# Gated linear attention and a hard-swish MLP in float32: signs of the second weight's slices taken by ScalarE, and a new order of all instructions

## The chip, the cores and the metric

The kernel runs on one core of a Trainium2 chip. The core has TensorE (PE in the profile) for matrix products, VectorE (DVE), ScalarE (ACT), GpSimd (POOL), and SyncE (SP), whose queue issues the transfers here. The metric is the device time of one execution in microseconds. The median of three runs of the kernel before is 535.52 us (535.26 to 536.10).

## What is computed

For every batch and head a 48 by 48 state decays row by row with alpha, takes in the outer product of k and v, and is read by q. The result, 3072 tokens of 384 numbers, goes through two weights with a hard-swish between them.

```python
batch, n_heads, seq, head_dim = (4, 8, 768, 48)
n_tokens, d_model, d_ff = (3072, 384, 2048)
...
for t in range(S):
    state = alpha[:, :, t, :, None] * state + np.einsum('bhd,bhe->bhde', k[:, :, t], v[:, :, t])
    y[:, :, t] = np.einsum('bhd,bhde->bhe', q[:, :, t], state)
...
x = np.ascontiguousarray(attn_out.transpose(0, 2, 1, 3)).reshape(B * S, H * D)
h = x @ w_in
relu6 = np.clip(h + 3.0, 0.0, 6.0)
g = h * relu6 / 6.0
return (g @ w_out).astype(np.float32)
```

The weights arrive as float64, that is as pairs of 32-bit words, and are made float32 on the chip.

## The kernel before

**Attention.** The sequence is cut into 24 chunks of 128 tokens (six for each batch). Chunk j has its loads `la`, `lk`, `lq`, `lv`; transposes `ta`, `tk`, `tq` (by TensorE for j below 6, by VectorE from then on); `ca` puts alpha in place; `r` and `p` are VectorE's scans that make the decay factors; `k` and `q` multiply by them. `kb` and `ck` turn k to token order (from chunk 8 on `kt`, `kw`, `kr` do it through memory), `sc` are the scores, `m` masks them, `qa` and `sv` place q and the state as extra rows, `u` is TensorE's update of the state, `sm` and `st` add it and decay it, `ya` and `yb` are the two halves of the output, `cy` copies it out as input for the MLP.

**The MLP.** Two chunks make a group of 256 tokens, twelve groups in all. Groups 0 and 1 use the weights as they are: `f`, or `fa` and `fb` for one chunk, is the first product, `fr` the clip on ScalarE, `fg` the multiplication on VectorE, `b` the second product in four parts (for group 0), `bo` and `so` its way out. From group 2 on the first product is formed from sums (`xc` of inputs, `y` of the first weight) in 20 products `M`, with `n`, `o`, `e`, `h` behind them; the second product is from group 1 on made of 7 products `P`, from sums `s` of its input and `x` of the second weight, with `K`, `G` and the store `O` behind them. `x.0` to `x.3` need all eight slices of the second weight; `P.1.3` reads what `x.1` writes, `P.1.2` what `x.2` writes. `z` are idle products of the identity matrix with itself.

**The weights.** Both come in 16 slices of 768 numbers for each of 128 partitions (768 KB each): 0 to 7 are the first weight, 8 to 15 the second. `w` loads a slice into one of five buffers of word pairs; three of these hold slices 8 to 15 in turn, so a later load waits until an earlier slice's `d4` has run. Then there are two ways (lines 173 to 217):

- Slices in `BY_HALVES` (0, 1, 2 and 4 before): ScalarE's `d1` rounds the low word, `dx` writes a float16 zero with the number's sign into the upper half of the low word, `d2` takes the magnitude times 2^16; VectorE's `d3` clamps it and shifts it left by 3; GpSimd's `d4` adds the low word.
- The other twelve: `d1` and `d2` without the factor, no `dx`; `d3` has a third step on VectorE (line 210) that combines sign and top bits of the high word with the shifted bits; `d4` adds the low word to that.

**The order.** Nothing orders the work but one string of some 1790 words, each a step, worked off by `run` (line 748 and on). Every engine, and SP's queue of transfers, takes its own instructions in the order of these words, and waits for what other engines must have finished.

Of the kernel before, what the change touches and what calls it, by code (L numbers as in the profile page):

```python
# [17 lines left out]
def kernel(  # L18
# [42 lines left out]
    G = 2  # L61
# [114 lines left out]
    BY_HALVES = {0, 1, 2, 4}  # L176
# [395 lines left out]
    for i in range(8):  # L572
        r, o = divmod(i, 3)
# [176 lines left out]
    with tc.manual_schedule():  # L750
        run("""z.0.5 z.0.3 z.0.1 z.0.8 qa.0.0 w.0 d2.0 d3.0 la.0 ta.0.0 ca.0 r.0 lk.0 tk.0.1 k.0
               z.0.2 p.0 la.1 ta.1.2 lq.0 tq.0.3 ca.1 r.1 lk.1 lv.0.0 sv.0.0 d1.0 kb.0.0 ck.0 z.0.2
               u.0.2.1 sm.0.0 sv.0.1 q.0 qa.0.1 tk.1.0 k.1 p.1 z.0.2 sc.0.2.3 m.0 la.2 ta.2.0 ca.2
               dx.0 w.2 d2.2 kb.1.0 ck.1 lq.1 r.2 sm.0.1 st.1 tq.1.2 q.1 d3.2 z.0.3 d1.2 dx.2 lv.1.1
               u.1.3.1 sv.1.0 sm.1.0 p.2 sm.1.1 sc.1.0.2 m.1 ya.0.3 yb.0 cy.0 lq.2 w.1 d1.1 tq.2.1
               q.2 d4.2 lk.2 tk.2.3 k.2 fa.2.0 d4.0 st.2 sc.2.0.2 d2.1 d3.1 m.2 dx.1 d4.1 qa.1.1
               lk.3 la.3 ta.3.1 ca.3 la.4 fa.0.1 sv.1.1 w.3 r.3 ta.4.3 ca.4 r.4 tk.3.1 k.3 kb.2.0
               qa.1.0 d2.3 ya.1.2 yb.1 cy.1 fa.1.2 lq.3 ck.2 d1.3 p.3 d3.3 lv.2.2 u.2.3.2 sm.2.0
               d4.3 fb.2 tq.3.1 q.3 fb.1 qa.2.0 sm.2.1 sv.2.0 st.3 fr.0.2.0 fg.0.2 lk.4 tk.4.0
               sv.2.1 w.5 d2.5 k.4 d3.5 d1.5 qa.3.0 d4.5 qa.2.1 sc.3.1.3 m.3 w.6 d2.6 d1.6 d3.6 d4.6  # L760
               lv.3.0 lq.4 w.7 kb.3.2 fb.0 f.0.3.3 kb.4.0 ya.2.1 ck.3 u.3.3.2 sm.3.0 fr.0.3.1 fg.0.3
               fr.0.1.0 fg.0.1 qa.3.1 sv.3.0 sm.3.1 p.4 d2.7 sv.3.1 d1.7 d3.7 d4.7 f.0.5.0 fr.0.5.1
               fr.0.0.0 fg.0.5 fg.0.0 tq.4.3 ck.4 la.5 ta.5.2 f.0.6.3 ca.5 w.4 d2.4 ya.3.0 yb.3 cy.3
               fr.0.6.1 yb.2 cy.2 w.9 d2.9 q.4 qa.4.1 d1.4 d1.9 dx.4 la.6 w.8 d3.4 r.5 lk.5 w.10
               d3.9 p.5 ca.6 fg.0.6 d4.9 w.12 lq.5 lv.4.1 d2.8 d3.8 f.0.7.2 d1.8 st.4 d4.8 d4.4 w.11
               fr.0.7.0 fg.0.7 f.1.7.0 fr.1.7.1 fg.1.7 sc.4.0.2 m.4 f.1.1.1 fr.1.1.0 fg.1.1 f.1.3.3
               fr.1.3.1 d2.10 d1.10 tk.5.3 f.1.0.2 d2.12 d3.10 d4.10 w.13 fg.1.3 fr.1.0.0 fg.1.0 k.5
               d3.12 lq.6 f.1.6.0 f.1.2.1 u.4.1.0 sm.4.0 d1.12 d4.12 sv.4.0 qa.4.0 ya.4.2 fr.1.6.1
               fg.1.6 w.15 tq.5.3 fa.4.3 sv.4.1 d2.11 kb.5.1 d2.13 fr.1.2.0 f.1.4.2 fr.1.4.1 d1.11
               sm.4.1 q.5 r.6 d3.11 d3.13 fg.1.4 d4.11 lv.5.0 lk.6 tq.6 p.6 d2.15 d3.15 fg.1.2 d1.13  # L770
               d4.13 sc.5.0.3 yb.4 f.1.5.0 fr.1.5.1 fg.1.5 tk.6 m.5 b.1.0.2 fb.4 b.1.1 d1.15 d4.15
               st.5 y.5 w.14 la.7 lk.7 cy.4 d2.14 qa.5.1 ck.5 b.0.0.1 fr.0.4.0 d3.14 k.6 q.6 ca.7
               fg.0.4 d1.14 d4.14 x.0 y.1 y.10 b.0.1 y.0 y.2 u.5.2 P.1.0.0 K.1.0 qa.5.0 sv.5.0
               qa.6.1 P.1.1.3 b.0.2 b.1.2 kb.6.0 ya.5.3 y.6 s.1.0.0 sm.5.0 sv.5.1 G.1.0.0 tk.7
               s.1.1.1 s.1.2.3 x.1 yb.5 cy.5 b.1.3 sc.6.1.2 lv.6.2 ck.6 u.6.3.0 s.1.3.2 x.2 P.1.2
               b.0.3 K.1.1 y.7 s.1.4 s.1.5 y.11 y.3 r.7 xc.2.1 x.3 y.4 y.8 xc.2.3 k.7 xc.2.0 xc.2.4
               y.9 y.12 y.16 y.13 y.15 P.1.3.3 K.1.2 P.1.4 bo.1 P.1.5 xc.2.5 G.1.1.1 P.1.6 y.14 y.17
               y.19 xc.2.6 sm.6.0 G.1.2.2 y.20 M.2.0.2 lv.12.1 la.8 O.1.1 O.1.0 ca.8 y.18 y.21 y.23
               so.1 G.1.3.3 n.2.0.8 bo.0 lq.7 lv.7.0 O.1.2 m.6 xc.2.2 xc.2.10 xc.2.7 tq.7 r.8 p.7
               xc.2.8 sv.6.1 M.2.15.3 M.2.1 kb.7.3 n.2.1.9 M.2.16 M.2.2 n.2.2.10 M.2.7.0 n.2.7.11  # L780
               sm.6.1 xc.2.9 q.7 p.8 M.2.3 M.2.4 n.2.4.12 M.2.8 o.2.0.0 M.2.5 n.2.5.13 qa.7.0 sv.6.0
               st.7 lk.8 O.1.3 lq.8 lk.9 la.9 la.10 tk.8 tq.8 lq.10 lq.9 ya.6.1 yb.6 M.2.9 z.1.3
               M.2.18.1 o.2.1.0 e.2.1.1 M.2.10 cy.6 ck.7 sc.7.0.2 u.7.1.3 n.2.10.14 M.2.11 qa.7.1
               ca.9 la.11 y.22 M.2.6.2 h.2.1 q.8 m.7 e.2.0.0 h.2.0 n.2.11.15 qa.6.0 n.2.18.10 qa.8.1
               M.2.12 M.2.19 n.2.12.12 M.2.13 sm.7.0 sv.7.1 r.9 k.8 o.2.3.0 sv.7.0 ya.7.0 y.24
               o.2.5.0 n.2.13.12 o.2.2.0 yb.7 cy.7 sc.8.1.2 xc.3.1 o.2.2.1 e.2.2.1 xc.3.3 o.2.3.1
               M.2.14 xc.3.4 xc.3.0 xc.3.5 o.2.4.0 xc.3.7 xc.3.6 o.2.6.0 P.2.0.1 M.3.0.2 M.2.17
               h.2.2 o.2.6.1 e.2.3.0 h.2.3 o.2.7.0 K.2.0 n.3.0.12 M.3.1 n.3.1.9 e.2.5.1 M.3.7.0
               n.3.7.13 xc.3.8 o.2.7.1 xc.3.2 kt.8 e.2.6.0 h.2.6 tk.9 M.3.2 n.3.2.10 e.2.4.0 P.2.1.3
               h.2.4 h.2.5 s.2.0.14 e.2.7.0 G.2.0.1 h.2.7 M.3.3 M.3.4 n.3.4.8 k.9 s.2.1.11 M.3.8  # L790
               o.3.0.0 ca.10 kt.9 P.2.3.3 s.2.2.15 s.2.3.14 lv.8.2 kw.8 kr.8 lk.10 sm.7.1 xc.3.9
               M.3.5 n.3.5.11 K.2.2 e.3.0.1 xc.3.10 M.3.9 o.3.1.0 P.2.2 K.2.1 u.8.0.3 M.3.18.2 s.2.5
               M.3.10 n.3.10.14 n.3.18.15 e.3.1.0 s.2.4 P.2.4 tq.9 h.3.0 st.8 sv.8.0 M.3.11 n.3.11.8
               tk.10 p.9 sm.8.0 q.9 r.10 k.10 qa.9.0 qa.9.1 m.8 sm.8.1 h.3.1 M.3.19 o.3.5.0 kt.10
               P.2.5 G.2.2.0 st.9 M.3.12 sc.9.0.1 qa.8.0 n.3.12.10 o.3.3.0 kw.9 lv.9.0 kr.9 sv.8.1
               u.9.2.3 sm.9.0 sv.9.1 sv.9.0 G.2.1.2 sm.9.1 st.10 M.3.15.2 M.3.16 M.3.6.3 M.3.13 m.9
               o.3.4.0 o.3.6.0 tq.10 n.3.13.10 o.3.2.0 e.3.4.1 ya.8.2 yb.8 ya.9.3 yb.9 cy.9 M.3.14
# [135 lines left out]
```

## Time and profile before

| what | value |
|---|---|
| median of three runs | 535.52 us |
| the profiled execution | 535.44 us |
| its span in the trace | 533.7 us |
| granted TensorE clock over the span | 1.0 |
| transfers | 54.40 MB, mean 102 GB/s |
| VectorE's clamps and shifts of the full path, lines 207 and 208 | 12 and 12, mean 703 and 605 ns |
| clamps and shifts of the path by halves, lines 203 and 205 | 4 and 4, mean 860 and 696 ns |
| ScalarE's rounding and magnitude, lines 186 and 196 | 935 and 929 ns |
| idle products, line 532 | 58 instructions for 29 pairs |

Times are counted from the start of the span. A float32 product of TensorE is two instructions, so 29 idle pairs are 58. Busy time of TensorE contains overlapped and modelled ends, so work is better counted from start to start. TensorE's first 34 instructions, idle products, begin at 1.46 and take 6.75 us; later ones follow each other at about 0.11.

### The profile page before, as it was taken

What the parts mean: (1) busy time and instruction counts of PE and PEld (TensorE: products, weight loads), DVE (VectorE), ACT (ScalarE), POOL (GpSimd) and SP (SyncE); (2) the same over time, 40 slices, a digit from 0 to 9 for tenths busy, and PEclk for the clock granted to TensorE, in tenths of its full rate; (3) what the DMA queues carried; (4) which work ended last, traced back from release to release, by engine and by line L of the source; (5) the groups of instructions that cost most, each with busy time, mean ns of one, the idle gap of its engine ahead of it and who ended that gap; (6) DMA issues with size and microseconds to landing.
All of it is one profiled execution on the core that took longest, in us unless ns stands there. A gap on an engine that the chain in (4) does not pass through costs nothing.

```text
span 533.7 us, 15143 instructions
## 1 busy us (share of the span) xinstructions
PE 524.6 (98%) x6306; PEld 499.4 (94%) x6306; DVE 477.2 (89%) x849; ACT 257.2 (48%) x503; POOL 50.4 (9%) x71
## 2 busy tenths in 40 slices
PE   8799999999999999999999999999999999999997
PEld 7698886789999999999999999999999999999997
DVE  6999989999999999998999999999999899496382
ACT  3889865212653553553544444642634544553340
POOL 5333425100000000000000000000000000000000
DMA  9998876005615155254344355044454042100001
GB/s 174 217 252 256 215 216 152 21 2 154 152 30 116 32 121 135 57 140 95 87 110 113 91 124 140 19 120 102 115 136 104 11 110 43 44 2 2 15 16 37
DMA packets 124100, 54.40 MB, mean 102 GB/s; under 512 B 83328, under 2 KB 116864, under 8 KB 124032
## 3 DMA queue, kind: packets, MB, share of 16 engines
q1 hardware_dynamic: 124032, 53.44, 42.5%
q8 instruction: 49, 0.80, 0.6%
q14 instruction: 19, 0.16, 0.1%
HBM read 44.50 MB, written 8.91 MB: 100 GB/s over the span
## 4 chain that ended last, share of the span: by engine, by line
PE 85%; DVE 8%; POOL 2%; DMA 2%; ACT 1%; issue 1%; SPq 1%; DVEq 0%; POOLq 0%
PE m_ps L703 34%; PE m_ps L600 34%; PE m_ps L478 5%; PE t_ps L455 4%; PE t_ps L346 2%; PE t_ps L429 2%; PE m_ps L489 2%; PE t_ps L282 1%; DVE rings L647 1%; DMA v<-in_v_dram 1%; DVE raw L537 1%; ACT raw L191 1%; DMA kq<-in_k_dram 1%; DVE g_sb L647 1%; DVE w L537 1%
## 5 line engine op out<-in xcount | busy, mean ns | idle before, releaser
L606 ACT COPY g_sb<-m_ps 128x512 f32<-128x512 f32 x110 | 63.6, 584 | 124.9 <-PE m_ps L600 104.1
L703 PE MATMUL m_ps<-w,g_sb 128*128 128x192 f32 x704 | 121.7, 327 | 0.0
L703 PEld LDWEIGHTS m_ps<-w,g_sb 128*128 128x128 f32 x704 | 113.7, 190 | 0.4
L703 PE MATMUL m_ps<-rings,g_sb 128*128 128x192 f32 x528 | 91.5, 326 | 0.0
L703 PEld LDWEIGHTS m_ps<-rings,g_sb 128*128 128x128 f32 x528 | 85.4, 190 | 0.1
L600 PE MATMUL m_ps<-xc,w 128*128 128x128 f32 x640 | 82.7, 277 | 0.3 <-DVE w L541 0.3
L600 PEld LDWEIGHTS m_ps<-xc,w 128*128 128x128 f32 x640 | 77.5, 192 | 1.5 <-issue 0.5
L494 ACT ACTIVATE r<-g_sb,half 128x512 f32<-128x512 f32 x80 | 56.8, 722 | 32.9 <-DVE g_sb L541 12.1
L498 DVE SCALAR_TENSOR_TENSOR g_sb<-r,g_sb 128x512 f32<-128x512 f32 x80 | 53.6, 682 | 4.6 <-ACT r L494 4.2
L600 PE MATMUL m_ps<-xT,raw 128*128 128x128 f32 x400 | 52.5, 277 | 0.0
L600 PEld LDWEIGHTS m_ps<-xT,raw 128*128 128x128 f32 x400 | 48.6, 192 | 0.6
L409 POOL TENSOR_TENSOR st<-sm,R 128x192 f32<-128x192 f32 x20 | 12.9, 643 | 353.8 <-DVE sm L439 306.7
L647 DVE TENSOR_TENSOR g_sb<-g_sb 128x512 f32<-128x512 f32 (+1 forms) x55 | 42.0, 795 | 0.2
L600 PE MATMUL m_ps<-xT,w 128*128 128x128 f32 x320 | 42.0, 276 | 0.0
L600 PEld LDWEIGHTS m_ps<-xT,w 128*128 128x128 f32 x320 | 39.3, 192 | 0.1
L366 ACT COPY A<-q 48x256 f32<-48x256 f32 x88 | 35.5, 404 | 5.0 <-DVE q L332 3.7
L356 DVE TENSOR_TENSOR A<-t_ps,mask 64x256 f32<-64x256 f32 x96 | 36.0, 414 | 0.4
L478 PE MATMUL m_ps<-xT,w 128*128 128x256 f32 x144 | 32.8, 382 | 0.0
L600 PE MATMUL m_ps<-xc,raw 128*128 128x128 f32 x240 | 31.8, 276 | 0.0
L309 DVE TENSOR_TENSOR_SCAN R<-t,ones 128x516 f32<-128x516 f32 x24 | 29.7, 1236 | 1.1 <-ACT t L300 1.0
L478 PEld LDWEIGHTS m_ps<-xT,w 128*128 128x128 f32 x144 | 26.7, 190 | 3.6
L600 PEld LDWEIGHTS m_ps<-xc,raw 128*128 128x128 f32 x240 | 29.6, 192 | 0.1
(104 smaller groups left out, 731.0 us busy)
## 6 DMA issues: line engine op xcount, KB each, us to landing
raw<-in_moe_w_out_dram SPq DMA_DIRECT2D x8, 768.0 KB, 5.2
raw<-in_moe_w_in_dram SPq DMA_DIRECT2D x6, 768.0 KB, 6.8
v<-in_v_dram SPq DMA_DIRECT2D x48, 96.0 KB, 3.0
out_dram<-oh SPq DMA_DIRECT2D x44, 96.0 KB, 1.7
far<-kq SPq DMA_DIRECT2D x64, 64.0 KB, 2.2
kb<-far SPq DMA_DIRECT2D x64, 64.0 KB, 2.0
aq<-in_alpha_dram SPq DMA_DIRECT2D x36, 96.0 KB, 2.5
qq<-in_q_dram SPq DMA_DIRECT2D x36, 96.0 KB, 2.4
```

Of the source, the lines that this page charges most:

```text
L309: nc.vector.tensor_tensor_scan(out=reverse(R, n - 1, n), data0=reverse(ax, n, n), data1=reverse(ones, n, n), initial=0.0, op0=ALU.mult, op ...
L356: nc.vector.tensor_tensor(out=to[:, a], in0=sc[a][half], in1=mask[half, half].unsqueeze(1).to_broadcast([HB, NP, HB]), op=ALU.mult)
L366: nc.scalar.copy(out=to[:, a], in_=Q_t[j][64 * a : 64 * a + D, :, half])
L409: nc.gpsimd.tensor_tensor(out=st, in0=sm, in1=R_t[j][:, :, 0:1].to_broadcast([C, NP, D]), op=ALU.mult)
L455: nc.tensor.matmul(y_of(j, (i + 1) // 2, p)[:, HB * b : HB * b + HB], vb[:, p, e : e + 32], A_t[j][:, b, 2 * p + a], start=(b == 0 and i = ...
L478: nc.tensor.matmul(h[:, f], w1[:, kk, o : o + C], xT_t[g][:, kk], start=(kk == 0), stop=(kk == KT - 1))
L494: nc.scalar.activation(out=to, in_=h, func=AF.Relu, bias=half, scale=1.0 / 6.0)
L498: nc.vector.scalar_tensor_tensor(out=to, in0=r, scalar=1.0, in1=h, op0=ALU.min, op1=ALU.mult)
L600: nc.tensor.matmul(acc[g][i][:, f * C : (f + 1) * C], spots[w][:, f * C : (f + 1) * C], x_of(g, x), start=(first and f == 0), stop=last, s ...
L606: nc.scalar.copy(out=slots[z], in_=acc[g][i])
L647: nc.vector.tensor_tensor(out=out, in0=in0, in1=in1, op=ALU.subtract)
L703: nc.tensor.matmul(to[g], a, rhs[:, f], start=(first and f == 0), stop=(last and f == HF - 1), skip_group_check=True)
```

## The change

`BY_HALVES` also takes in slices 8 to 15, and the whole order string is another one. The steps and their numbers are the same, but for eight `dx` more; `d3` of slices 8 to 15 has two steps where it had three, and their `d4` reads another operand. The arguments behind a step's chunk or group, which choose a bank or a slot, differ too. The parts of the two strings that the text speaks of:

```diff
-    BY_HALVES = {0, 1, 2, 4}
+    BY_HALVES = {0, 1, 2, 4, *range(8, 16)}
...
-        run("""z.0.5 z.0.3 z.0.1 z.0.8 qa.0.0 w.0 d2.0 d3.0 la.0 ta.0.0 ca.0 r.0 lk.0 tk.0.1 k.0
-               z.0.2 p.0 la.1 ta.1.2 lq.0 tq.0.3 ca.1 r.1 lk.1 lv.0.0 sv.0.0 d1.0 kb.0.0 ck.0 z.0.2
-               u.0.2.1 sm.0.0 sv.0.1 q.0 qa.0.1 tk.1.0 k.1 p.1 z.0.2 sc.0.2.3 m.0 la.2 ta.2.0 ca.2
-               dx.0 w.2 d2.2 kb.1.0 ck.1 lq.1 r.2 sm.0.1 st.1 tq.1.2 q.1 d3.2 z.0.3 d1.2 dx.2 lv.1.1
-               u.1.3.1 sv.1.0 sm.1.0 p.2 sm.1.1 sc.1.0.2 m.1 ya.0.3 yb.0 cy.0 lq.2 w.1 d1.1 tq.2.1
-               q.2 d4.2 lk.2 tk.2.3 k.2 fa.2.0 d4.0 st.2 sc.2.0.2 d2.1 d3.1 m.2 dx.1 d4.1 qa.1.1
-               lk.3 la.3 ta.3.1 ca.3 la.4 fa.0.1 sv.1.1 w.3 r.3 ta.4.3 ca.4 r.4 tk.3.1 k.3 kb.2.0
-               qa.1.0 d2.3 ya.1.2 yb.1 cy.1 fa.1.2 lq.3 ck.2 d1.3 p.3 d3.3 lv.2.2 u.2.3.2 sm.2.0
-               d4.3 fb.2 tq.3.1 q.3 fb.1 qa.2.0 sm.2.1 sv.2.0 st.3 fr.0.2.0 fg.0.2 lk.4 tk.4.0
...
-               d4.13 sc.5.0.3 yb.4 f.1.5.0 fr.1.5.1 fg.1.5 tk.6 m.5 b.1.0.2 fb.4 b.1.1 d1.15 d4.15
-               st.5 y.5 w.14 la.7 lk.7 cy.4 d2.14 qa.5.1 ck.5 b.0.0.1 fr.0.4.0 d3.14 k.6 q.6 ca.7
-               fg.0.4 d1.14 d4.14 x.0 y.1 y.10 b.0.1 y.0 y.2 u.5.2 P.1.0.0 K.1.0 qa.5.0 sv.5.0
...
+        run("""z.0.2 z.0.2 z.0.8 z.0.3 qa.0.0 w.0 d2.0 d1.0 la.0 ta.0.0 ca.0 z.0.2 z.0.3 dx.0 lk.0
+               z.0.5 lq.0 tq.0.1 tk.0.2 la.1 ta.1.3 ca.1 d3.0 r.0 p.0 k.0 q.0 qa.0.1 r.1 kb.0.0 ck.0
+               sc.0.2.3 m.0 w.1 d1.1 d2.1 dx.1 lv.0.0 u.0.1.0 sm.0.0 sv.0.1 sv.0.0 d4.0 lk.1 tk.1.2
+               lq.1 tq.1.3 k.1 kb.1.1 ck.1 la.2 lv.1.1 sm.0.1 st.1 sv.1.0 ya.0.2 yb.0 cy.0 u.1.0.1
+               p.1 q.1 qa.1.0 sc.1.2.3 qa.1.1 d3.1 d4.1 sm.1.0 m.1 ta.2.0 fa.0.0 sm.1.1 w.5 d2.5
+               d3.5 sv.1.1 d1.5 ca.2 r.2 d4.5 st.2 ya.1.2 yb.1 cy.1 w.2 d2.2 d1.2 dx.2 d3.2 d4.2
+               lk.2 la.3 p.2 fa.1.1 fb.0 fb.1 fr.0.1.0 tk.2.3 k.2 fg.0.1 fr.0.0.1 fg.0.0 ta.3.1 ca.3
+               lq.2 tq.2.0 q.2 w.4 d2.4 d3.4 d1.4 dx.4 r.3 d4.4 f.0.5.2 fr.0.5.0 qa.2.1 w.6 d1.6
+               d2.6 sc.2.2.3 m.2 kb.2.1 fa.2.3 lk.3 tk.3.0 k.3 p.3 d3.6 d4.6 fb.2 la.4 ta.4.2 ca.4
...
+               w.10 d2.10 d3.10 fr.1.5.1 fg.1.5 p.5 w.3 lv.4.1 sv.4.0 d2.3 d3.3 d1.3 f.1.0.0 f.1.1.2
+               ck.4 u.4.2.1 sm.4.0 sc.4.0.3 m.4 w.8 d2.8 d3.8 d1.10 d1.8 dx.8 f.1.6.1 fr.1.6.0
+               fg.1.6 la.6 ca.6 lk.5 lq.5 tk.5.2 tq.5.0 q.5 d4.9 w.12 fr.1.1.1 d2.12 f.1.2.3 la.7
+               ca.7 k.5 lv.5.2 lk.7 d4.3 fg.1.1 sm.4.1 f.1.3.1 dx.10 fr.1.2.0 fg.1.2 d3.12 r.6 d1.12
+               dx.12 fr.1.0.1 lk.6 tk.6 fg.1.0 kb.5.3 d4.8 w.11 b.1.0.2 d4.10 d4.12 ck.5 u.5.0 d2.11
+               fr.1.3.0 d1.11 w.13 la.9 st.5 d3.11 d2.13 la.8 w.15 lq.6 dx.11 d4.11 w.14 lq.7 fg.1.3
+               r.7 sc.5.1.2 tk.7 f.0.3.3 fr.0.3.1 m.5 fg.0.3 k.6 f.1.7.0 fr.1.7.0 d2.15 qa.4.0 d1.15
+               f.1.4.1 fr.1.4.1 b.0.0.3 kb.6.3 b.0.1 b.1.1 p.6 d3.13 fg.1.7 d3.15 s.1.1.1 fg.1.4
+               ca.8 dx.15 d4.15 d1.13 qa.4.1 tq.6 d2.14 d3.14 y.5 s.1.0.0 y.3 y.9 s.1.2.3 s.1.3.2
+               s.1.4 q.6 y.6 dx.13 d4.13 y.8 y.7 P.1.0.0 d1.14 dx.14 d4.14 x.0 qa.5.0 qa.5.1 b.1.2
+               b.1.3 lv.6.0 sv.4.1 sv.5.0 K.1.0 sm.5.0 sv.5.1 y.1 tq.7 p.7 x.1 lk.8 lq.9 y.2 x.2 y.0
+               P.1.1.1 s.1.5 x.3 ya.4.1 yb.4 cy.4 ya.5.2 yb.5 cy.5 bo.1 xc.2.1 ck.6 y.10 y.15 xc.2.0
+               y.11 y.4 y.13 y.16 xc.2.3 b.0.2 P.1.3.2 K.1.2 P.1.2 b.0.3 K.1.1 P.1.4 xc.2.2 xc.2.4
```

## The prediction

> **What bounds the kernel now.** I read the page's busy shares first, then the busy time by stage, then who TensorE waited for, then the groups of the weight steps, then VectorE and GpSimd beside each other in the stage that the change touches.
>
> ```profile
> span 533.7 us, 15143 instructions
> PE 524.6 (98%) x6306; PEld 499.4 (94%) x6306; DVE 477.2 (89%) x849; ACT 257.2 (48%) x503; POOL 50.4 (9%) x71
> ```
>
> TensorE is busy 98% of the span, VectorE 89%, ScalarE 48%. By stage (columns: length, then busy time of TensorE, its weight loads, VectorE, ScalarE, GpSimd, granted clock, DMA):
>
> ```profile
> 0.00:31.00 31.00, 25.04 (x376) 22.13 (x376) 25.98 (x48) 20.63 (x31) 14.03 (x25) 1.00 1.11 206
> 31.00:80.00 49.00, 49.00 (x668) 42.95 (x665) 46.59 (x77) 40.66 (x68) 16.67 (x16) 1.00 0.87 232
> 80.00:126.00 46.00, 46.00 (x348) 36.31 (x347) 45.66 (x68) 12.11 (x25) 8.58 (x14) 1.00 0.28 67
> 126.00:513.00 387.00, 386.71 (x4814) 380.52 (x4813) 349.77 (x644) 181.06 (x375) 11.15 (x17) 1.00 0.36 86
> 513.00:533.70 20.70, 17.82 (x110) 17.53 (x108) 9.24 (x16) 2.78 (x7) 0.00 (x0) 1.00 0.07 24
> ```
>
> TensorE's idle time is 6.0 us before 31 us, 0.3 in the middle and 2.9 at the end, 9.1 in all. VectorE is a close second: 45.66 of 46 us between 80 and 126. The change neither adds nor removes a matmul, so the time can only fall where TensorE waits or turns on idle matmuls, in the first 31 us, and can only rise through new waits. Of the head's waits the largest are
>
> ```profile
> PE m_ps L532 <- POOL ident masks.py:199: 1.5, 1, 1.5
> PE t_ps L429 <- issue: 1.2, 2, 1.0
> PE t_ps L455 <- DVE s L439: 0.7, 1, 0.7
> ```
>
> The second is the state update waiting for values that land at 20.0 us.
>
> **The edit to slices 8 to 15.** Here are its groups: VectorE's combining step, ScalarE's sign step, GpSimd's add on the two paths.
>
> ```profile
> L210 DVE SCALAR_TENSOR_TENSOR raw<-raw,w 128x768 uint32<-128x768 uint32 x11 | 10.6, 960 | 0.5
> L191 ACT ACTIVATE raw<-raw 128x768 f16<-128x768 int32 x3 | 5.8, 1941 | 0.1
> L217 POOL TENSOR_TENSOR w<-raw 128x768 int32<-128x768 int32 x11 | 17.7, 1608 | 32.4 <-DVE raw L210 15.2 <-ACT raw L186 6.7 <-issue 4.3
> L217 POOL TENSOR_TENSOR w<-w,raw 128x768 int32<-128x768 int32 x3 | 5.7, 1929 | 3.0 <-ACT raw L191 3.0
> ```
>
> VectorE loses eight L210: one starts at 91.32 and its successor at 92.19, so 0.87 each, 7.0 us. The clamp and the shift stay; on this layout they start 0.58 and 0.60 apart (90.14, 90.72, 91.32). ScalarE gains eight signs at 1.94: 15.5 us. GpSimd's add goes from 1.61 to 1.93: 2.6 us. No DMA is added, but the reload of a buffer waits for the add, and now the add for the sign.
>
> VectorE's 7.0 us are not on TensorE's path (no wait after 31 us but 0.3), so I book them as nothing gained, only as slack. ScalarE's 15.5 us lie under TensorE: between 80 and 126 us ScalarE works 12.1 of 46. Without that cover they would cost up to 15.5. The first four signs fall between 50 and 72, where it has less room: 40.7 of 49 are taken between 31 and 80. The tight place is the last three slices. In the new order ScalarE, after the clip of f.1.4, runs dx.15, d1.13, qa.4.1, d2.14, dx.13 before GpSimd's d4.13: 1.94+0.93+0.8+0.91+1.94 = 6.5 us, with the clip 7.2 and the add 9.1. TensorE meanwhile has b.0.0, kb.6, b.0.1, b.1.1 and P.1.0, that is four times 2.6 and 0.5 = 10.9, before b.1.2 needs that slice: 1.8 us of cover. A sign may overlap its neighbours as L186 does (starts 0.82 apart for 0.93), which adds half a microsecond.
>
> The Trainium skill, "ScalarE: Activation LUTs", section Rules for kernel authors, would keep such simple arithmetic on VectorE, which speaks against the edit; the same page's section What ACT_TABLE_LOAD costs gives 186 ns plus 0.833 ns an element, an estimate of 0.83 us for 768. The row says 1.94, and the row decides; by the page's figure the eight signs would be 6.6 us and the cover some 2 us larger.
>
> **The lock.** Two rows show what GpSimd's add does to VectorE:
>
> ```profile
> 92.80 1.95 DVE L332 TENSOR_TENSOR q<-q,P 128x512 f32<-128x512 f32 x1
> 92.51 1.69 POOL L217 TENSOR_TENSOR w<-raw 128x768 int32<-128x768 int32 x1 [3.76 <-DVE raw L210]
> ```
>
> The multiplication takes 0.68 elsewhere (the one before it at 92.19); here it ends when the add does, 1.27 late. The clamp at 82.47 took 1.78 instead of 0.55 beside the add of 81.81 to 83.83: 1.23. Steps that read PSUM ran beside adds without loss (L498 x2 at 85.81, 1.28, beside the add at 86.03). So the old order paid twice, 2.5 us. Bounds for the new: no add met, a gain of 2.5; all eight met for a whole add, 15.4. Laid against VectorE's neighbours in the new order, d4.9, d4.11, d4.15, d4.13 and d4.14 stand among steps that read SBUF twice or were held, the other three beside PSUM reads or transposes; I take five at about 1.2, 6 us.
>
> **The head.** I follow the new order queue by queue with the old rows. Only 30 idle matmuls stand before the first transposes, not 34 (6.75 us together, the last at about 0.11): they start 0.4 earlier, at 7.5. VectorE: r.0 8.7 to 10.1, then p.0, k.0, q.0 (1.1+0.6+0.6) to 12.5, r.1 to 13.9, m.0 to 15.4. On SP's queue w.1 is moved past lv.0, lk.1, lq.1, la.2 and lv.1. In the old run loads landed 1.2 us apart for 192 KB and 2.2 for a slice (la.2 13.83, w.2 16.01, lq.1 17.19). So lv.0 lands at about 13.7 instead of 13.0, which meets ck.0 (13.9, behind qa.0.1), and lv.1 between 18.3 and 20, as before, because lq.2, w.2 and others moved behind it. Update 1 thus starts at 20.0, sc.1 ends near 21.1. VectorE then has m.1 1.5, sm.1.1 0.3, d3.5 2.2, r.2 1.4, d3.2 1.4, p.2 1.1 and k.2, fg.0.1, fg.0.0, q.2 at 0.6: 10.3 from 21.2, to 31.5; TensorE, through fa.0, attention 1, fa.1, fb.0, fb.1, three transposes and f.0.5, is there at 31.9 for sc.2.
>
> The old order stood at fb.2 at 33.85. Against it the new one has then done f.0.5 (2.6) and one more fa or fb (1.34), and lacks two transposes, a kb, a sc, u.2 and one idle pair: 0.9+0.5+0.5+0.6+0.2 = 2.7. It is ahead by 3.9-2.7 = 1.2 in work and by 1.95 in time: 3.2 us. I left out hand-offs between engines, some 0.1 each (k.0 ends 11.20, kb.0 starts 11.35; ck.0 12.59, u.0 12.69), about eight on this chain: 0.8. Gain 2.4. Bounds: none of it, if lv.1 and w.1 land 2.4 later; 3.2 with hand-offs hidden.
>
> The skill's "TensorE: Matmul & The Clock Gate", section What's actually happening, says that an idle window of about 3.4 us halves the clock. The longest wait in my layout is 1.4 us, so by the rule nothing happens, though the new order has no idle matmuls between 10 and 30 us; no row here shows a fall.
>
> **Does VectorE keep up?** From q.2 (31.5) to x.1 its rows sum to 69 us: x.1 is ready at 100.3 plus lateness. TensorE has 72 us from 31.9 to P.1.3, which needs x.1, plus 1 us that the old order lost between groups over that stretch: 105. Cover 4.9. The old order's VectorE was 3.8 late there (2.5 of locks, 1.3 waiting for u.4). With 3.8 no stall; with my 6, a stall of 1.1. I take half, 0.5. Later steps have more room than the old order left, since VectorE has 7 us less before it.
>
> Sum: -2.4 +0.5 = -1.9 us. The end stays at 2.9 us. The profiled execution took 535.44 (span 533.7 and 1.7 around it), 0.1 below the median 535.52: **533.5 us**.
>
> **Rivals.** *Gain given back* (0.18): VectorE is 7.3 late at x.1, TensorE stalls 2.4 there: 535.4. For it: its 99% between 80 and 126; against: 7 us less work. *Locks decide* (0.15): all eight adds meet VectorE at the measured 1.27, 10.2 us late, a stall of 5.3 against 2.4: 538.3. It turns slower from 7.3 us of lateness on. For it: each add is 0.3 longer and the last three lie among two-input steps; against: three adds sit beside PSUM reads. *Signs late* (0.07): ScalarE reaches dx.13 and dx.14 6 us later than laid out, b.1.2 waits 4.2: 537.7. For it: ScalarE's 40.7 of 49 between 31 and 80, and the old d2.14 waited 3.4 for its slice; against: it idled between 90 and 126, and any lateness up to 1.8 is free. *It does not do what it says* (0.05): the head's loads land late and nothing is won, 535.5.
>
> **Chances.** Forecast 0.55, at 531.5 to 534.8 alone. Less than 0.2% (1.07 us) is what a measurement can't tell from no change. Faster 0.62 (forecast, and a part of the first rival), same 0.14, slower 0.24. The range 531.5 to 537.5 leaves out the worst of the locks.
>
> **What would show it.** Eight L191 more and eight L210 fewer; sc.2 near 32 us; TensorE's waits before 31 us; any TensorE wait on L647 (x.1), L217 or L191 between 60 and 126 us; two-input VectorE rows of 1.9 us. A TensorE wait after 126 us, which I exclude, would make the prediction wrong.

## The result, and the profile after

The changed kernel takes 536.88 us in the median of 20 runs (535.05 to 539.69), the kernel before 535.56 beside it (20 runs, 535.25 to 536.62). The ratio is 1.0024, with a 95% interval of 1.001 to 1.0038: slower by a little more than what a measurement of this kernel can tell from no change. The forecast was 533.5 and faster; 536.88 lies inside its range, on the wrong side of no change.

The profiled execution took 539.69 (span 537.9), the longest of the twenty. So its waits are at the upper end; a second profiled execution of the same kernel took 537.41 and is set beside it below.

The busy shares, the stages (cut as in the prediction, the last 20.7 us again by themselves) and two groups of the page of after:

```profile
span 537.9 us, 15113 instructions
...
PE 524.2 (97%) x6306; PEld 500.1 (93%) x6306; DVE 475.2 (88%) x841; ACT 270.7 (50%) x511; POOL 56.9 (11%) x71
...
L217 POOL TENSOR_TENSOR w<-w,raw 128x768 int32<-128x768 int32 x11 | 22.2, 2016 | 30.8 <-ACT raw L191 21.8 <-DVE g_sb L498 4.4 <-ACT v L419 1.9
...
L191 ACT ACTIVATE raw<-raw 128x768 f16<-128x768 int32 x11 | 21.2, 1928 | 0.1
```

```profile
0.00:31.00 31.00, 24.81 (x376) 22.98 (x377) 24.17 (x44) 21.54 (x31) 15.49 (x25) 0.89 1.10 236
31.00:80.00 49.00, 49.00 (x618) 42.96 (x618) 44.41 (x73) 42.65 (x64) 20.34 (x22) 1.00 0.89 211
80.00:126.00 46.00, 41.57 (x302) 31.69 (x302) 43.14 (x60) 22.92 (x36) 8.13 (x6) 1.00 0.34 84
126.00:517.20 391.20, 391.02 (x4907) 384.97 (x4906) 355.32 (x654) 180.93 (x375) 12.97 (x18) 1.00 0.36 82
517.20:537.90 20.70, 17.82 (x110) 17.52 (x108) 8.19 (x14) 2.63 (x7) 0.00 (x0) 1.00 0.12 38
```

The edit did what it says: eight sign steps more on ScalarE, eight fewer steps on VectorE. TensorE is idle 6.2 us before 31 us (6.0 before the change), none to 80, 4.4 between 80 and 126 (none before the change), 0.2 to the end stage (0.3) and 2.9 there, as before. Two things are new: the granted clock is 0.89 in the head, and TensorE stops between 80 and 126. Who it waited for, first up to 40 us, then from 40 to 126:

```profile
PE t_ps L455 <- issue: 2.5, 1, 2.5
PE m_ps L532 <- POOL ident masks.py:199: 1.5, 1, 1.5
```

```profile
PE m_ps L516 <- POOL w L217: 3.3, 2, 2.6
PE t_ps L455 <- ACT v L419: 0.7, 1, 0.7
PE m_ps L703 <- DVE w L647: 0.4, 1, 0.4
```

**The first place, the head.** TensorE's timeline in the changed kernel:

```profile
23.16 0.99 PE L455 MATMUL t_ps<-A,v 128*32 128x64 f32 x55
26.61 0.33 PE L455 MATMUL t_ps<-A,v 128*32 128x64 f32 x9 [2.46 <-issue]
26.87 5.92 PE L489 MATMUL m_ps<-xT,w 128*128 128x128 f32 x36
...
36.62 0.69 PE L346 MATMUL t_ps<-q,k 48*64 48x64 f32 x32
```

In the middle of yb.1, with nine of its 64 matmuls left, TensorE stands for 2.5 us and waits for nothing that the profile shows. The trace's transfers of kind "instruction" point to the reason: TensorE's program comes in pieces of 16 KB, 49 of them for its 12,700 instructions (matmuls, weight loads and its queue's own steps, counted together). In the kernel before, the second piece of the span starts at 22.64, when TensorE starts its 521st instruction (22.61). In the changed kernel the 521st starts at 20.72, but the transfer at 23.81, 3.1 us later; the stop comes behind the 705th. Then fa.1, fb.0 and fb.1 take 5.92 us for 36 matmuls, 0.16 apiece where earlier ones took 0.12 (1.50 for twelve): the granted clock is 0.5 from 16.66 to 20.08 and from 26.90 to 30.32. The kernel before has 1.0 throughout. sc.2 starts at 36.62, where the prediction had 31.9.

**The second place, b.1.2 and b.1.3.** SP's queue, ScalarE, GpSimd and TensorE in the changed kernel:

```profile
73.03 0.98 SPq L166 DMA_DIRECT2D raw<-in_moe_w_out_dram  x2
74.11 7.56 SPq L262 DMA_DIRECT2D aq<-in_alpha_dram  x8
81.85 0.39 SPq L166 DMA_DIRECT2D raw<-in_moe_w_out_dram  x1
```

```profile
88.86 0.91 ACT L196 ACTIVATE w<-raw 128x768 f32<-128x768 f32 x1 [3.76 <-DMA raw<-in_moe_w_out_dram]
...
91.49 0.66 ACT L494 ACTIVATE r<-m_ps,half 128x512 f32<-128x512 f32 x1
92.06 1.92 ACT L191 ACTIVATE raw<-raw 128x768 f16<-128x768 int32 x1
...
96.21 1.92 ACT L191 ACTIVATE raw<-raw 128x768 f16<-128x768 int32 x1
```

```profile
98.21 2.27 POOL L217 TENSOR_TENSOR w<-w,raw 128x768 int32<-128x768 int32 x1 [2.25 <-ACT raw L191]
100.86 1.87 POOL L217 TENSOR_TENSOR w<-w,raw 128x768 int32<-128x768 int32 x1 [0.38 <-ACT raw L191]
```

```profile
96.46 1.45 PE L516 MATMUL m_ps<-w,g_sb 128*128 128x384 f32 x4
100.53 1.56 PE L516 MATMUL m_ps<-w,g_sb 128*128 128x384 f32 x4 [2.62 <-POOL w L217]
102.78 2.85 PE L516 MATMUL m_ps<-w,g_sb 128*128 128x384 f32 x8 [0.69 <-POOL w L217]
```

Read it from the top. SP issues the eight small loads of la.9 and la.8, which takes it 7.56 us, ahead of slice 15 (the trace books 3.3 of these us as waits for a slice's load to land); the buffer for slice 15 had been free since 78.1 (the end of d4.12). So slice 15 is issued at 81.85, and ScalarE, which takes its steps in order, stands 3.76 us in front of d2.15. Behind d2.15 stand the clip of f.1.4 (91.49), dx.15 (92.06) and dx.13 (96.21). GpSimd's d4.13 follows at 98.21, and TensorE, done with its other work at 97.9, waits 2.6 us and then 0.7 more for d4.14.

### The profile page after: what moved, and what is told of

It is laid out like the page before. It is cut to its first block, busy times and chain, and to the rows that moved or that the text cites. A ratio compares the mean times of both kernels' runs of the same rounds, so it can differ in the third digit from the quotient of the medians.

```text
span 537.9 us, 15113 instructions
## 1 busy us (share of the span) xinstructions
PE 524.2 (97%) x6306; PEld 500.1 (93%) x6306; DVE 475.2 (88%) x841; ACT 270.7 (50%) x511; POOL 56.9 (11%) x71
## 4 chain that ended last, share of the span: by engine, by line
PE 85%; DVE 6%; DMA 4%; POOL 1%; issue 1%; SPq 1%; ACT 1%; DVEq 0%; ACTq 0%; POOLq 0%
PE m_ps L703 34%; PE m_ps L600 34%; PE t_ps L455 4%; PE m_ps L478 3%; PE m_ps L489 2%; PE t_ps L429 2%; PE t_ps L346 2%; DMA aq<-in_alpha_dram 1%; DMA rings<-in_q_dram 1%; DMA qq<-in_q_dram 1%; PE t_ps L282 1%; DVE rings L647 1%; DVE raw L539 1%; DVE g_sb L647 1%; DVE w L537 1%
## 5 line engine op out<-in xcount | busy, mean ns | idle before, releaser
L600 PE MATMUL m_ps<-xc,w 128*128 128x128 f32 x640 | 82.8, 277 | 0.0
L600 PEld LDWEIGHTS m_ps<-xc,w 128*128 128x128 f32 x640 | 77.7, 192 | 0.8
L600 PE MATMUL m_ps<-xT,raw 128*128 128x128 f32 x400 | 52.1, 277 | 0.0
L409 POOL TENSOR_TENSOR st<-sm,R 128x192 f32<-128x192 f32 x20 | 14.8, 742 | 339.2 <-DVE sm L439 220.4
L600 PEld LDWEIGHTS m_ps<-xT,raw 128*128 128x128 f32 x400 | 48.5, 192 | 0.5
L600 PE MATMUL m_ps<-xT,w 128*128 128x128 f32 x320 | 41.8, 276 | 0.0
L600 PEld LDWEIGHTS m_ps<-xT,w 128*128 128x128 f32 x320 | 39.1, 192 | 0.3
L537 DVE TENSOR_TENSOR g_sb<-g_sb 128x512 f32<-128x512 f32 x40 | 27.4, 690 | 7.0 <-ACT g_sb L606 6.8
L600 PE MATMUL m_ps<-xc,raw 128*128 128x128 f32 x240 | 32.1, 277 | 0.0
L600 PEld LDWEIGHTS m_ps<-xc,raw 128*128 128x128 f32 x240 | 29.7, 192 | 0.3
```

What stands on the lines that cost most here:

```text
L409: nc.gpsimd.tensor_tensor(out=st, in0=sm, in1=R_t[j][:, :, 0:1].to_broadcast([C, NP, D]), op=ALU.mult)
L537: eng.tensor_tensor(out=out, in0=in0, in1=in1, op=ALU.add if s1 > 0 else ALU.subtract)
L600: nc.tensor.matmul(acc[g][i][:, f * C : (f + 1) * C], spots[w][:, f * C : (f + 1) * C], x_of(g, x), start=(first and f == 0), stop=last, s ...
```

## The experiments

Times are medians of 5 to 12 runs, ratios are to runs of the kernel before beside them, with 95% intervals. Below, "loads behind" is the first edit here; later kernels build on it.

### The change again, and three parts of it

The changed kernel, as it is:

> The changed kernel once more, for a second profile and its scatter. Theory 1 (the head): the 2.5 us wait inside yb.1 at 24 to 26.5 us has no semaphore behind it and ends 2.8 us after a fetch of TensorE's program began, late, among the loads of slices 5 and 2; such a wait varies from run to run, so it should be 0 to 3 us here, and with it the time, 535 to 540. Theory 2 (the signs): the wait of b.1.2 and b.1.3 for GpSimd's adds, 3.3 us together near 100 us, is a matter of queues and should be here again at 2.5 to 4. Rival (locks): TensorE waits for x.1 (0.4 us in the first profile) grow to over 2.

536.97 us, ratio 1.0025 (1.0006 to 1.0044). The profiled execution (537.41) has both places: 2.2 us without a releaser in yb.1, a program transfer 2.9 us after the 521st instruction, clock 0.5 from 27.16 to 30.58 alone, and 1.0 us of waits for L217 in place of 3.3. So the two places are there in both executions, in changing sizes. Such changes would also explain the spread of 535.05 to 539.69 in the changed kernel, where the one before spreads over 1.4; the last kernels below, which have neither place at its full size, spread over 0.8 at most, in five runs each.

Only SP's order changed at the second place:

```diff
-  fr.1.3.0 d1.11 w.13 la.9 st.5 d3.11 d2.13 la.8 w.15 lq.6 dx.11 d4.11 w.14 lq.7 fg.1.3
+  fr.1.3.0 d1.11 w.13 st.5 d3.11 d2.13 w.15 la.8 lq.6 dx.11 d4.11 w.14 lq.7 la.9 fg.1.3
```

> The changed kernel with two words of SP's queue moved: la.9 behind lq.7, la.8 behind w.15, so that w.15 no longer stands behind eight transfers. Theory 2: w.15 is issued as soon as d4.12 is done (78 instead of 82 us), d2.15 no longer holds the clip of f.1.4 for 3.8 us, dx.13 and dx.14 come 3 us sooner, the wait of b.1.2 and b.1.3 falls from 3.3 to below 0.8, and the time by 2.5 to 3.3 us against the changed kernel, to 533.5 to 535. Rival (locks): VectorE is what is late, the wait moves on to x.1 in P.1.3 and less than 1 us is won.

534.77 us (532.55 to 536.16), ratio 0.998 (0.9967 to 0.9993), 2.1 us below the change. ScalarE now has slice 15 at 84.40, and b.0.1 to b.1.3 run as one stretch:

```profile
84.40 0.92 ACT L196 ACTIVATE w<-raw 128x768 f32<-128x768 f32 x1 [1.11 <-DMA raw<-in_moe_w_out_dram]
```

```profile
95.77 5.46 PE L516 MATMUL m_ps<-w,g_sb 128*128 128x384 f32 x16
```

No wait for L217 is left. Eight small transfers at a wrong place in one queue cost more than the 1.3 us by which the change is slower than the kernel before.

The edit without the new order (the old string, with each dx of slices 8 to 15 put just ahead of its d4):

```diff
-    BY_HALVES = {0, 1, 2, 4}
+    BY_HALVES = {0, 1, 2, 4, *range(8, 16)}
...
-  d4.8
+  dx.8 d4.8
```

> The old order, with slices 8 to 15 on the path by halves: each new sign stands right before its add, nothing else is moved. If the edit itself is harmless, TensorE waits nowhere after 31 us and the time stays within 0.7 us of the old 535.5. Theory 2 (ScalarE has no room between 31 and 80 us, 40.7 of 49 us taken): five signs of 1.9 us in that stretch make it late, TensorE waits for clips or adds, and the time is 536 to 540. Rival (locks): VectorE is 7 us shorter, so faster scans and sums; nothing for TensorE, 535.0 to 535.6.

539.66 us, ratio 1.0071 (1.0059 to 1.0083). TensorE waits 1.3 for ScalarE's qa behind the signs, 0.7 for VectorE's fg and 1.0 at L600 after 126 us; these are 3.0 of the 4.1 lost. Another 0.6 is lost at u.2, which waits for its load of v near 34 us, ahead of all the new signs. Signs squeezed into the old order are a loss: ScalarE's 15.5 us are not free wherever they are put.

The new order without the edit (slices 8 to 15 on the full path, their eight dx left out):

> The new order with the old path for slices 8 to 15: their eight signs are left out and VectorE's third step is back. Theory 1: the head is the same, so the same scatter, 0 to 4 us. Theory 2: ScalarE has 15.5 us less, the adds of d4.13 and d4.14 are no longer late, no wait of b.1.2. Rival (locks and VectorE): VectorE has 7 us more to do before x.1, TensorE waits 2 to 5 us at P.1.3 and after, 537 to 541.

540.17 us, ratio 1.0091 (1.0078 to 1.0104), 3.2 above the change. VectorE, with its 7 us back, makes TensorE wait in front of b.0.0:

```profile
87.54 4.54 PE L516 MATMUL m_ps<-w,g_sb 128*128 128x384 f32 x8 [2.29 <-DVE g_sb L498]
```

The wait is only a part of it: eight such matmuls take half of 5.46 above and 4.54 here, because the granted clock is 0.5 from 88.18 to 91.59, behind the wait. So the order and the edit need each other: in this order the 7 us of VectorE that the prediction booked as slack are slack that is used.

### The second place by another engine

In the changed kernel with SP's order as it was, slice 13's rounding and sign go ahead of d2.15, and its add behind its shift:

```diff
-  fr.1.7.0 d2.15 qa.4.0 d1.15
+  fr.1.7.0 d1.13 dx.13 d2.15 qa.4.0 d1.15
...
-  d3.13 fg.1.7
+  d3.13 d4.13 fg.1.7
```

> The changed kernel with the rounding and the sign of slice 13 (d1.13, dx.13) taken ahead of d2.15 on ScalarE, and its add d4.13 right behind its shift; SP's queue as in the change. Theory (ScalarE takes its steps in order, and d2.15 stands waiting 3.76 us for a slice that SP issued late, with slice 13's sign behind it): the wait of b.1.2 for the add, 2.6 us, goes; b.1.3 still waits for slice 14, 0 to 1.5 us; 534.3 to 536.0, against 536.9. Rival (only SP's order matters, ScalarE's does not): both waits stay and the time is that of the change, 536.4 to 537.4. Rival (GpSimd's add of slice 13 now meets VectorE's k and p steps at 85 to 88 us, and the lock gives the gain back): the waits go, VectorE's rows there grow by 1.2 each, and x.1 waits 1 us or more; 536 or above.

535.08 us (533.0 to 537.48), ratio 0.9991 (0.9978 to 1.0004), 1.8 below the change. Both waits for L217 are gone, x.1 waits 0.4 as before. The lock of the last rival did come, but without its price: beside the moved add (86.51, 1.87) a clamp of VectorE took 1.94, where another in that stretch took 0.53 (85.15), and TensorE did not wait for it.

```profile
86.86 1.94 DVE L203 TENSOR_SCALAR w<-w 128x768 f32<-128x768 f32 x1
```

The mechanism at the second place is shown from two sides: a late slice, and an in-order engine with a due step behind it.

Both mends together:

> The kernel with la.9 and la.8 moved behind and slice 13's sign first, and nothing else. Each of the two took the waits of b.1.2 and b.1.3 away by itself. Theory (they mend the same place): together they give no more than the better one, 534.2 to 535.2, with 1 to 2.5 us without a releaser in yb.1 as before. Rival (each mends a different loss): 532.2 to 533.7.

535.24 us (533.38 to 537.97), ratio 0.9995 (0.9981 to 1.0008): no more than either alone. The head's wait was 2.3 us in the profiled execution.

### The head

SP takes slice 2 behind lq.2 and behind slice 6, which waits for d4.1; on top of "loads behind":

```diff
-  cy.1 w.2 d2.2 d1.2 dx.2 d3.2 d4.2 lk.2 la.3 p.2
+  cy.1 lk.2 la.3 lq.2 w.6 w.2 d2.2 d1.2 dx.2 d3.2 d4.2 p.2
```

> The kernel with la.9 and la.8 moved behind, in which SP also issues slice 2 behind lq.2 and behind slice 6, whose buffer comes free only when d4.1 ends near 21.9 us; no other engine's order changes. Theory (TensorE's program fetch is due when some 520 of its instructions have started, near 20.4 us, but stands 2.4 us behind the loads of slices 5 and 2): the transfers run out before 20.5, the fetch starts within 0.5 us of that point, the wait in yb.1 with no releaser, 1.9 us, falls below 0.5, and with it the halved clock at 26 to 29 us; 531.0 to 533.2, against 534.8. Rival (the fetch is late because TensorE runs through short instructions, loads or not): it starts near 22.9 again, the wait stays at 1.5 to 2.5 us, time 534.3 to 535.3. Rival (the wait goes and VectorE is the bound behind it): the wait goes, x.1 or sc.2 waits that much more, 534.0 or above.

537.46 us, ratio 1.0027 (1.0012 to 1.0042). The time rose, yet the head answers. The program transfer starts at 22.08, the wait is 1.3 instead of 1.9, the clock stays at 1.0, the 36 products take 4.29 instead of 5.79, and TensorE is 2.5 us ahead at 31 us. All of it is lost at the next step, which waits for VectorE, and VectorE for slice 2 (a further 2.1 us against "loads behind" go between 40 and 100 us, in small waits that were not traced):

```profile
35.97 0.69 PE L346 MATMUL t_ps<-q,k 48*64 48x64 f32 x32 [2.48 <-DVE q L332]
```

```profile
30.80 0.69 DVE L203 TENSOR_SCALAR w<-w 128x768 f32<-128x768 f32 x1 [4.38 <-ACT w L196]
```

Seven idle pairs at TensorE's waits in the head, on top of "loads behind" (`z.1.2` ahead of kb.0, u.0 and tk.1, `z.1.1` ahead of tq.1):

> The kernel with la.9 and la.8 moved behind, and seven idle pairs put where TensorE waits in the head: two each ahead of kb.0, u.0 and tk.1, one ahead of tq.1. Theory (the clock halves for 3.41 us after a stretch of 3.41 us in which TensorE was busy for about 2.1 of it; more busy time keeps it): no granted clock under 1.0 between 15 and 20 us, kb.1 and ya.0 at their full rate, 0.5 to 1.3 us less, 533.5 to 534.3 against 534.8. The second halving at 26 to 29 us stays, as does the wait for the program fetch. Rival (the halving does not follow from TensorE's busy share): it stays, and the time is 534.5 to 535.5. Rival (the halving goes, but the loads of chunk 1 set the pace): clock 1.0 and the same time within 0.3.

535.24 us, ratio 0.9994 (0.9981 to 1.0008). The halving at 15 to 19 us is gone, the one at 26.07 and the 2.3 us in yb.1 stay, and the time is not lower: the rival with the loads setting the pace there fits. It is not a clean test, though: a stop of 0.5 us without a releaser is new in ya.0, so the price of the first halving stays open.

The two and slice 13's sign together:

> The three edits on top of la.9 and la.8 moved behind: slice 13's sign first, slice 2 later on SP's queue, seven idle pairs in the head. If the three costs are separate and all on the path: no wait in yb.1 without a releaser, clock 1.0 from 7 us on, no wait of b.1.2 or b.1.3, time 529.8 to 532.5, faster than every kernel so far. If VectorE takes over as the bound at x.1: a wait there of 1 to 3 us and 532.5 to 534.5. If the idle pairs bring the program fetch to a worse place: the wait in yb.1 comes back, 534 or above.

536.9 us, ratio 1.0022 (1.001 to 1.0034), a miss. Against "loads behind" TensorE was 3.2 us ahead at 31 us and then waited 2.9 for q.2; after this the clock was 0.5 from 35.17 to 42.00, and by then another 2.9 were lost.

Now slice 2 has to come late for SP and still in time for ScalarE. It takes slice 1's buffer (free when d4.1 ends), and slice 6 the one that it leaves; with "loads behind" and slice 13's sign first:

```diff
-    HOMES = [0, 1, 2, 3, 4, 0, 1, 2] + [(i + 3) % 3 for i in range(NW - NW1)]
+    HOMES = [0, 1, 1, 3, 4, 0, 2, 1] + [(i + 3) % 3 for i in range(NW - NW1)]
...
-  cy.1 w.2 d2.2 d1.2 dx.2 d3.2 d4.2 lk.2 la.3 p.2
+  cy.1 lk.2 la.3 lq.2 w.2 d2.2 d1.2 dx.2 d3.2 d4.2 p.2
```

> The kernel with la.9 and la.8 moved behind and slice 13's sign first, in which slice 2 takes the buffer of slice 1 (free when d4.1 ends near 22) and is issued behind lq.2, and slice 6 takes the buffer that slice 2 had. So the transfers of the head pause near 20.5 us, and slice 2 still lands near 25, before ScalarE wants it at 26. Theory (the late program fetch and the halved clock cost the head, and VectorE's wait in the run with slice 2 later came of that slice alone): the program fetch starts before 22, the wait without a releaser is 1.3 us or less, the clock stays at 1.0 from 20 to 35 us, and sc.2 starts between 33.2 and 34.6 instead of 35.95; 531.3 to 533.3. Rival (VectorE holds the head anyway): sc.2 waits 1.5 us or more for q.2 again and starts after 35; 534.0 to 535.5. Rival (the gain in the head is taken back at x.1): x.1 waits 1.5 us or more; 533.5 to 535.

536.13 us, ratio 1.0009 (1.0 to 1.0017). Against "loads behind" TensorE is 3.0 us ahead at 31 us and 1.9 at 36, sc.2 starts at 34.1; and 1.7 behind at 77. The expectation had no such case. The trace names it: slice 7 now had the buffer that slice 9 needs, so that slice 9 waited for d4.7 (47.8) instead of d4.6 (45.0), and the loads behind it were late for ScalarE, VectorE and then TensorE:

```profile
47.81 0.37 SPq L166 DMA_DIRECT2D raw<-in_moe_w_out_dram  x1
```

```profile
74.28 0.66 PE L374 MATMUL t_ps<-ident,k 128*128 128x128 f32 x4 [1.33 <-DVE k L332]
```

The same with the idle pairs:

> The same kernel with the seven idle pairs in the head on top. Theory (the halving at 15 to 19 us costs little, because the loads of chunk 1 set the pace there): no halving there, the time within 0.5 us of the kernel without the pairs. Rival (it costs its full 1 us): 0.7 to 1.3 us less. Rival (the pairs bring the program fetch to a worse place): the wait without a releaser grows by 0.5 or more, and the time by as much.

537.53 us, ratio 1.0037 (1.0025 to 1.0049): 1.4 slower than without the pairs. yb.1 has no stop left (it was 0.4 without the pairs); there is one of 1.4 in ya.0, and another of 0.5 at 229 us:

```profile
20.37 0.31 PE L455 MATMUL t_ps<-A,v 128*32 128x64 f32 x4 [1.40 <-issue]
```

The wait without a releaser grew, as the last rival has it, but it is not what the time went to: sc.2 starts at 34.10, against 34.06 without the pairs. Where the 1.4 us went stays open, but for the 0.5 at 229 us.

These stops stand at fixed places of the program, not of the time. In all twelve profiled executions that stop in yb.1 it is behind TensorE's 705th or 706th instruction. The stops in ya.0 are behind the 450th, and the one at 229 us behind the 5569th, that is 255 or 256 instructions earlier and 19 times 256 later; 49 pieces for 12,700 instructions are about 259 for each.

To measure the program transfer alone, SP holds slices 5 and 2 both behind slice 6 (with "loads behind" and slice 13's sign first, on the old buffers):

> The kernel with la.9 and la.8 moved behind and slice 13's sign first, in which SP holds both slice 5 and slice 2 behind slice 6, so until d4.1 has ended near 21 us: nothing but small loads is under way when TensorE has started some 520 instructions. It measures the program fetch; its time is not meant to be good, since slice 5 comes late. Theory (the fetch is late because loads stand ahead of it): it starts within 0.5 us of the start of instruction 520, near 20.4, and TensorE has no wait without a releaser of more than 0.3 us in yb.1. Rival (the fetch follows a fixed count or time of its own): it starts 1.8 us or more after that instruction again, and the wait is 1 us or more. Time by both: 536 to 541, from waits for slices 5 and 2 on VectorE and ScalarE.

540.86 us, ratio 1.0097 (1.0082 to 1.0111), from a wait of 6.9 us for sv.1.1, which stands behind slice 5 on ScalarE. The program transfer started at 21.67, 0.6 us after the 521st instruction. Over the kernels (starts of the 521st instruction and of the transfer):

```
kernel                  521st   transfer  late   wait in yb.1
before                  22.61   22.64     0.0    none
changed                 20.72   23.81     3.1    2.5
changed, again          20.69   23.58     2.9    2.2
loads behind            20.57   23.00     2.4    1.9
slice 2 later           20.19   22.08     1.9    1.3
slices 2 and 5 later    21.05   21.67     0.6    not seen (it stood for sv.1.1)
slice 7 moved (below)   20.67   21.59     0.9    0.3
```

The fewer loads stand ahead, the earlier it starts, and the wait follows its lateness: over the twelve executions that stop in yb.1 it is 0.5 to 0.8 us shorter. 0.6 us of lateness stay even with both slices held.

Last, slice 7 in the buffer of slices 0 and 5, so that slice 9 no longer waits for it (slice 8, which takes this buffer next and is loaded after slice 9, does: d4.7 ends at 47.57, its load is issued at 47.59):

```diff
-    HOMES = [0, 1, 1, 3, 4, 0, 2, 1] + [(i + 3) % 3 for i in range(NW - NW1)]
+    HOMES = [0, 1, 1, 3, 4, 0, 2, 0] + [(i + 3) % 3 for i in range(NW - NW1)]
```

> The kernel with la.9 and la.8 moved behind, slice 13's sign first and slice 2 in slice 1's buffer, but with slice 7 in the buffer of slices 0 and 5, so that slice 9's load no longer waits for d4.7. Theory (the head's loss counts in the end, and the 3.3 us given back between 55 and 77 us came from slice 9's late load alone): slice 9 is issued before 45.5, sc.2 starts near 34.2, TensorE keeps at least 1.3 us of its lead over the run with la.9 and la.8 moved behind up to 105 us, and the time is 532.3 to 533.9. Rival (the middle is bound by the transfers of slices 8 to 13 whatever the head does): the lead is gone by 77 us again, and the time is 534.3 to 535.5. Rival (the lead lasts to 80 us and VectorE at x.1 takes it): x.1 waits 1.3 us or more instead of 0.4, 534 to 535.

532.56 us (532.04 to 532.74), ratio 0.9938 (0.9925 to 0.995): faster than both kernels, and the spread is 0.7 us. The page and the head of it:

```profile
span 531.0 us, 15113 instructions
...
PE 522.2 (98%) x6306; PEld 498.5 (94%) x6306; DVE 474.4 (89%) x841; ACT 270.5 (51%) x511; POOL 58.1 (11%) x71
```

```profile
24.50 0.33 PE L455 MATMUL t_ps<-A,v 128*32 128x64 f32 x9 [0.34 <-issue]
24.75 4.29 PE L489 MATMUL m_ps<-xT,w 128*128 128x128 f32 x36
...
33.85 0.69 PE L346 MATMUL t_ps<-q,k 48*64 48x64 f32 x32 [0.91 <-DVE q L332]
```

The stop is 0.34 instead of 2.46, the products run at full clock, sc.2 starts 2.8 us earlier than in the changed kernel, and the 2 us gained on "loads behind" by 36 us are still 1.8 at 95 us; at the end of the span it is 2.5 (531.0 against 533.5).

The same without slice 13's sign moved:

> The same kernel with slice 13's sign where the change has it. If TensorE's lead of the head lasts, it reaches b.1.2 some 1.5 us earlier than in the run with la.9 and la.8 moved behind, where no wait was left there but little room; theory: b.1.2 waits 0 to 1.5 us for d4.13, the time 0 to 1.5 us above the kernel with the sign moved. Rival (moving the sign costs VectorE a lock and gains nothing): no wait there and the time the same or up to 0.6 below.

532.53 us, ratio 0.9941 (0.9927 to 0.9955), no wait at b.1.2: with slice 15 in time the sign's place does not matter. So the fastest kernel is the change with la.9 and la.8 moved behind, slice 2 behind lq.2, and slices 2, 6 and 7 in other buffers; "loads behind" alone is already below both, by 0.2% below the kernel before.

## Why the prediction was wrong

**Right.** The edit's own prices: eight L191 at 1.93, VectorE's seven microseconds as no gain by themselves (the edit alone was slower), no wait of TensorE after 126 us but 0.2. The stall at x.1 was taken as 0.5 and was 0.4, but that is luck: it is 0.41 to 0.44 in all fourteen profiled executions of the new order, whether TensorE comes there at 107.5 or at 116.6 us, so it does not measure the cover of 4.9; and in the changed kernel TensorE waits another 0.7 us just ahead of it, at 110.39, which the prediction did not have. The locks were put at five adds and 6 us; four VectorE steps were drawn out, and by less:

```profile
59.53 1.66 DVE L203 TENSOR_SCALAR w<-w 128x768 f32<-128x768 f32 x1
...
85.44 1.20 DVE L332 TENSOR_TENSOR k<-k,R 128x512 f32<-128x512 f32 x1
...
98.68 2.35 DVE L539 TENSOR_TENSOR raw<-w 128x512 f32<-128x512 f32 x1
101.06 2.21 DVE L541 SCALAR_TENSOR_TENSOR w<-w 128x512 f32<-128x512 f32 x1
```

Against 0.55 and 0.68 undisturbed that is 1.1, 0.5, 1.7 and 1.5, 4.8 in all. "Locks decide", with 10.2 us and a stall of 5.3, is out.

**First failed step: "1.8 us of cover" at the tight place.** The sum of ScalarE's work after the clip of f.1.4 was right in its rows. What failed is its start: the clip was laid where TensorE ends f.1.4 (85.7) and ran at 91.49, because d2.15 ahead of it waited for a load. The text asked of this stretch how long ScalarE works, not what stands ahead of it on ScalarE, and not what stands ahead of slice 15 on SP. The rival "Signs late" had the place and the mechanism (ScalarE 6 us late, b.1.2 waiting 4.2) and got 0.07. That wait was measured at 3.3 us in the one execution and 1.0 in the other; taking it away gained 2.1 and 1.8.

**Second failed step: "Gain 2.4" in the head.** The layout followed the waits between engines and the order of the loads, but not the one load that is in no queue of the program: TensorE's own instructions. sc.2 at 36.62 instead of 31.9 is 4.7 us; of these 2.5 are the stop in yb.1, and 1.6 the 36 products that took 5.92 instead of 4.29. The rest, 0.6, is hand-offs and loads. By the prediction's own count, 1.2 us of work ahead of fb.2, the step that should have gained 2.4 lost 1.4 (36.62 less 33.98 less 1.2). The bounds of that step, "none of it" to 3.2, had late loads alone in view and no loss at all. (fb.2 starts at 33.98 in the view; the prediction's 33.85 and its landing times are 0.13 too early, which changes nothing here.)

**The clock.** "The longest wait in my layout is 1.4 us, so by the rule nothing happens" does not hold. In the changed kernel the window of 3.41 us ahead of 16.66 held no wait above 0.7, TensorE was busy for 1.7 of it, and the clock fell for 3.41 us; ahead of 26.90 it was busy for 1.0. The Trainium skill's page "TensorE: Matmul & The Clock Gate", section What's actually happening, names an idle window of about 3.4 us as what halves the clock. The measurement decides: a window that is idle in part is enough. Take all windows of 3.41 us at full clock, laid out from the changes of the clock in each profiled execution. Every one with under 1.3 us of busy time was followed by a halved clock, none with over 2.2; between 1.4 and 2.2 some were and some were not, and what decides there stays open.

**The sum.** With SP's queue changed and three slices in other buffers, the kernel takes 532.5, 1.0 below the forecast: what made the change a loss was two transfers that came late, slice 15's and that of TensorE's program. That this lies near 533.5 is partly luck. sc.2 still starts at 33.85 there, 1.95 later than laid out: VectorE waits 1.8 us for slice 2 and ends q.2 at 33.79 instead of 31.5. By the prediction's count that is a gain of 1.3 in the head, not 2.4; the span is 2.7 us shorter than before the change (531.0 against 533.7), and where the rest came from was not traced.

## What to carry to other kernels

When an order is laid out by hand, follow the slowest queue first: for each wait of an in-order engine ask what stands behind the waiting step, and for each late load what the issuing queue did just before it. A TensorE that runs through hundreds of short instructions while the transfers are full may stop for its own program; here the sign was a stop without a releaser in the middle of a group of equal matmuls, at the same instruction in every execution that had it. A gain early in the kernel lasts only if no buffer is handed over later than before: check who had the buffer last whenever one is reassigned.

## What the runs showed of the hardware

- A fetch of TensorE's program waits among data transfers: 0.6 us late with the slices held back, up to 3.1 with two slices under way, and a stop of up to 2.5 us. The stops lie 255, 256 or 19 times 256 instructions apart.
- The clock halves in steps of 3.41 us (6.83 and 10.24 in two executions). In the changed kernel it did so with no wait above 0.7 us in the 3.41 ahead, and it costs what runs in it: 36 products 5.92 instead of 4.29 us.
- SP needed 7.56 us to issue the eight loads of la.9 and la.8 (80 and 96 KB each) while two slices were under way, 3.3 of them waiting by the trace; four such loads took 1.89 us at 85.23 in "loads behind". A queue's issue time is itself a cost.
